# The last two superblocks: products laid out chunk by chunk, summed to one tap group, and transposed by a DMA

## The chip, the cores and the metric

The kernel runs on one core of one Trainium2 chip. The metric is the device time in microseconds, as a median over several runs; lower is better. Profile times are those of one profiled execution.

## The reference

A dynamic convolution over tokens, followed by a two-layer network without gates:

```python
# x: (8, 4096, 192), weight_gen: (8, 4096, 8, 7): 8 heads of 24 channels, 7 taps
w = softmax(weight_gen, axis=-1)                       # one weight per token, head and tap
x_unf = 7 tokens ending at each token, zeros ahead of the first one
conv = np.einsum('bshk,bskhg->bshg', w, x_unf)         # 32768 tokens x 192
h = conv @ w_in                                        # 192 x 2048
out = (h - np.tanh(h)) @ w_out                         # 2048 x 192, float32
```

## The kernel before

The 32768 tokens are cut into 32 superblocks of 1024 (`TOK`), numbered n = 0 to 31. Within a superblock partition p holds `J` = 8 neighbouring tokens, so a tap's products are 8 x 192 = 1536 elements on each of 128 partitions. The 192 channels are split over `NC` = 3 chunks of `R` = 64 rows each: channel d = 3u + c is row u of chunk c.

A superblock passes through these stages:

- *Softmax.* ScalarE takes the exponential of the weights, VectorE sums, inverts and scales them into `wsm`.
- *Products* (`products`, and its inner `mul` and `rest`). GpSimd multiplies x by the weights: taps 0 to 3 into the tile `pa` (two instructions, one less token block for taps 0 and 1, which VectorE does in `help`), then taps 4 to 6 into `pb` (one instruction). Products are bf16, written in the order of x: token, then channel.
- *Sums by DMA* (`dma_sum`, issued from GpSimd's queue, adding in the destination). The first adds `pb` to three tap groups of `pa`. From superblock 13 on (`TWO_SUMS`), `second_sum` adds two of the remaining four groups to the other two. It is issued in the next superblock's turn, between that one's `pa` and `pb` products; that of the last superblock comes right behind its first sum.
- *Transposes* (`transposes`, `conv_sums`, `conv_out`). TensorE multiplies each remaining tap group, 64 rows by 64 columns at a time, by an identity, adding the groups up in PSUM (`pc`, line 384): with two groups 32 matmuls for chunks 0 and 1, and 16 for chunk 2. ScalarE evicts the two results to `convT` (line 410).
- *First matmul* (`gemm1`, line 427). For each of 16 tiles f of the 2048 hidden units, 6 matmuls of 512 columns into `ph`; ScalarE takes the tanh of it into `th` (line 440), VectorE writes `ph - th` to `gt` (line 441).
- *Second matmul* (`out_stream`, line 495). It lags by one superblock: 8 output blocks of 16 pairs of matmuls each go to two PSUM banks, and ScalarE evicts each block (`store_out`, line 514); SyncE stores a superblock's result in one DMA (line 518). The last superblock's second matmul runs at the end (`gemm2_last`).

The order on every engine is written out by hand: TensorE and the others follow the loop over n and f at the end of the code. A plan for n says how many output pairs follow each tile f (`pairs`), and behind which tile, after how many pairs, the transposes of superblock n+1 are put (`t2` for chunks 0 and 1, `t1` for chunk 2):

```python
STEADY = dict(pairs=(5, 11, 0, 16, 4, 12, 6, 10, 0, 6, 10, 8, 8, 8, 8, 16), t1=(14, 8), t2=(13, 0), scale=14, sums=(1, 13))
```

In turn n GpSimd makes the products of superblock n+2 (`pa` at f = 1, `rest` at f = 3), so superblock 30 is multiplied in turn 28 and 31 in turn 29. Loads of x and of the weights and the stores are DMAs of SyncE's queue. `pa` has three buffers, `pb` one, `convT` two, and `ph` and `pc` share three.

Of the kernel before, what the change touches and what calls it, by code (L numbers as in the profile page):

```python
# [9 lines left out]
BF16 = mybir.dt.bfloat16  # L10

ACT = mybir.ActivationFunctionType
# [4 lines left out]
def kernel(  # L17
# [8 lines left out]
    nc = tc.nc  # L26

    B, S, D = x.shape
    H, K = weight_gen.shape[2], weight_gen.shape[3]
    G = D // H  # L30
    F = moe_w_in.shape[1]
    P = nc.NUM_PARTITIONS
    R = P // 2
    HALO = K - 1

    J = 8
    TOK = P * J
    JH = J // 2
    HT = TOK // 2
# [3 lines left out]
    NC = D // R  # L43
    KA, KH = 4, 2
    PART = (2, 3)
    TWO_SUMS = (13, 14, 15, 16, 17, 18, 19, 20, 21, 22, 23, 24, 25, 26, 27, 28, 29, 30, 31)
    AHEAD = 4
    STORE_FIRST = 8
    EXTRA = (5, 9, 11, 13)
# [17 lines left out]
    cpool = ctx.enter_context(tc.tile_pool(name="cpool", bufs=2))  # L67
# [24 lines left out]
    prods_of = {}  # L92
    to_sum = {}
    conv_of = {}
    g_of = {}
    last_act = {}
    probe = {}
# [96 lines left out]
    def softmax_norm(n, bank):  # L194

        wsm = softmax_tile()
        zr_v = bank[:, 512 - J * H : 512]
        nc.vector.reciprocal(zr_v, zsum_of[n][:])  # L198

        def finish():  # L200
            scale(nc.vector, wsm[:], e_of[n], zr_v)

        wsm_of[n] = (wsm, None, None, None)
        return finish
# [30 lines left out]
    def dma_sum(out, in_):  # L235
        return nc.gpsimd.dma_start(  # L236
            out=out.rearrange("p k j d -> p k (j d)"),
            in_=in_.rearrange("p k j d -> p k (j d)"),
            accum_op=mybir.AluOpType.add,
            max_dma_last_dim=2 * J * D,  # L240
        )

    def help(n, ph, j):

        if n not in held:
            held[n] = (x_of[n], wsm_of[n][0], papool.tile([P, KA, J, D], BF16, name="pa"))
        x_t, wsm, pa = held[n]
        x_v = x_t[:]
        w = ph[:, 0, 0 : KH * H].rearrange("p (k h) -> p k h", k=KH)
        nc.vector.tensor_copy(w, wsm[:, j].rearrange("p h k -> p k h")[:, 0:KH])  # L250
        nc.vector.tensor_mul(  # L251
            pa[:, 0:KH, j, :].rearrange("p k (h g) -> p k h g", h=H),
            bass.AP(
                tensor=x_v.tensor,
                offset=x_v.offset + j * D,
                ap=[x_v.ap[0], [D, KH], [G, H], [1, G]],
            ),
            w.rearrange("p k (h o) -> p k h o", o=1).to_broadcast([P, KH, H, G]),
        )

    def products(n, taps=None, sums=None, hooks={}):

        x_t = x_of.pop(n)
        wsm, wsm_v, e_t, zr = wsm_of.pop(n)
        if e_t is not None:
            scale(nc.gpsimd, wsm[:], e_t, zr[:])

        pa = held[n][2] if n in held else papool.tile([P, KA, J, D], BF16, name="pa")
        held[n] = (x_t, wsm, pa)
        if n == 1:  # L270

            last = [opool.tile([P, 2, J, D], BF16, name="pb1", tag="out_sb") for _ in range(2)]
            home = [(pa, 0, KA), (last[0], KA, KA + 2), (last[1], KA + 2, K)]
        else:
            pb = pbpool.tile([P, K - KA, J, D], BF16, name="pb")
            home = [(pa, 0, KA), (pb, KA, K)]
        x_v = x_t[:]
        step = x_v.ap[0]

        def prod(k0, k1):  # L280
            for t, a, b in home:
                if a <= k0 and k1 <= b:
                    return t[:, k0 - a : k1 - a]

        def mul(eng, k0, k1, j0=0, j1=J):

            if eng is nc.scalar:
                for j in range(j0, j1):
                    for h in range(H):
                        eng.activation(  # L290
                            out=prod(k0, k1)[:, 0, j, h * G : (h + 1) * G],
                            in_=x_t[:, k0 + j, h * G : (h + 1) * G],
                            func=ACT.Copy,
                            scale=wsm[:, j, h, k0 : k0 + 1],
                        )
                return
            w = wsm_v if eng is nc.vector else wsm[:]
            nj = j1 - j0
            return eng.tensor_mul(  # L299
                prod(k0, k1)[:, :, j0:j1].rearrange("p k j (h g) -> p k (j h) g", h=H),  # L300
                bass.AP(
                    tensor=x_v.tensor,
                    offset=x_v.offset + (k0 + j0) * D,
                    ap=[step, [D, k1 - k0], [G, nj * H], [1, G]],
                ),
                w[:, j0:j1]
                .rearrange("p j h (k o) -> p k (j h) o", o=1)[:, k0:k1]
                .to_broadcast([P, k1 - k0, nj * H, G]),
            )

        def parts(*ks):
            return [[prod(k, k + 1)[:, 0] for k in ks]] * NC

        if taps is not None:
            for eng, k0, k1, j0, j1 in taps:
                m = mul(eng, k0, k1, j0, j1)
                if eng is nc.vector:
                    tap_of.setdefault((n, k0), m)
                if j1 == 1:
                    first_halo[0] = m  # L320
                if k0 in hooks:
                    hooks[k0]()
            prods_of[n] = parts(*sums)
            return

        nt = len(HELP.get(n, ()))
        first = mul(nc.gpsimd, 0, KH, 0, J - nt)
        if n in PACED:

            order(first, pace_of[n - 3], "pace")  # L330
        if n in LAST_TAP:

            x_after[n + 1] = mul(nc.gpsimd, KH, KA - 1)
            second_sum(n - 1)
        else:
            mul(nc.gpsimd, KH, KA)
            second_sum(n - 1)
        if n not in LAST_TAP or n not in X_LATE:
            x_after[n + 1] = first

        def rest():
            if n in PART:
                dma_sum(pa[:, 0:2], pa[:, 2:4])
            mul(nc.gpsimd, KA, K)
            if n in PART:
                prods_of[n] = parts(4, 5, 6, 0, 1)
            else:
                dma_sum(pa[:, 0:3], pb[:, 0:3])
                if n in LAST_TAP:
                    mul(nc.gpsimd, KA - 1, KA)  # L350
                if n in TWO_SUMS:
                    to_sum[n] = pa
                    prods_of[n] = parts(0, 1)
                else:
                    prods_of[n] = parts(3, 0, 1, 2)
                if n == NTOT - 1:
                    second_sum(n)

        return rest

    def second_sum(n):

        if n in to_sum:
            pa = to_sum.pop(n)
            dma_sum(pa[:, 0:2], pa[:, 2:4])

    def conv_sums(n, parts, pcs, home=None):

# [154 lines left out]
    pairs = out_stream()  # L523
# [68 lines left out]
    for c in range(NC):  # L592
# [16 lines left out]
        sums=(6, 5, 4, 3, 0, 2, 1),  # L609
# [17 lines left out]
    if SOFT_EARLY:  # L627
# [6 lines left out]
        sums=(0, 1, 4, 5, 6, 2, 3),  # L634
# [19 lines left out]
    for f in range(NFT):  # L654
# [9 lines left out]
        if f == EARLY[0][0]:  # L664
            pcs = []
            sums = conv_sums(1, ((0, 1),), pcs, obank)
# [15 lines left out]
    STEADY = dict(pairs=(5, 11, 0, 16, 4, 12, 6, 10, 0, 6, 10, 8, 8, 8, 8, 16), t1=(14, 8), t2=(13, 0), scale=14, sums=(1, 13))  # L682
    FIRST = dict(pairs=(4, 12, 0, 16, 1, 15, 0, 16, 0, 16, 0, 13, 3, 0, 16, 16), t1=(15, 2), t2=(11, 10), scale=15, sums=(1, 2, 3, 4, 8, 10))
    APART = dict(pairs=(4, 12, 0, 16, 0, 16, 4, 12, 0, 16, 4, 12, 0, 6, 10, 16), t1=(15, 5), t2=(10, 2), scale=15, sums=(7, 10))
    APART_IN = ()
    DOUBLE = dict(pairs=(4, 12, 0, 16, 0, 16, 5, 11, 0, 5, 11, 6, 10, 0, 16, 16), t1=(15, 4), t2=(11, 4), scale=15, sums=(1, 10))
    DOUBLE_IN = (4, 5, 6, 7, 8, 9, 10, 11)

    def transposes(n, chunks):
        pcs = []  # L690
# [16 lines left out]
    for n in range(1, NTOT):  # L707
        more = n < NTOT - 1
        finish = []
        plan = FIRST if n == 1 else DOUBLE if n in DOUBLE_IN else APART if n in APART_IN else STEADY  # L710

        soft = [m for m in (n + 3 if n <= AHEAD else n + 4,) if m < NTOT]
        for f in range(NFT):
            ph = gemm1(n, f)
# [37 lines left out]
            for chunks, at in sorted((((0, 1), plan["t2"]), ((2,), plan["t1"])), key=lambda c: c[1]):  # L752
                if more and at[0] == f:
                    out_pairs(at[1] - done)
                    done = at[1]
                    pc = transposes(n + 1, chunks)
                    if chunks == (2,):
                        finish = [softmax_norm(m, pc[:, 0]) for m in soft]
            if f >= plan["scale"]:
                for scale_one in finish:  # L760
                    scale_one()
                finish = []
# [42 lines left out]
```

## Time and profile before

| What | us |
|---|---|
| median of 3 runs | 746.24 (745.77 to 746.59) |
| span of the profiled execution (its own time from first to last instruction) | 743.4 |
| TensorE busy in it | 722.3 (97%) |
| VectorE, ScalarE, GpSimd busy | 687.4, 638.8, 654.5 |
| granted TensorE clock, mean | 0.995 of full speed |
| one matmul of line 427, of line 495 (duration, overlapping its neighbours) | 0.379, 0.243 |
| the chain that ended last | TensorE 92%, VectorE 5%, the rest 3% |

Matmuls are pipelined, so their durations overlap; the chain of waits, which gives how far each group moves the end, shows 0.65 us for the 6 matmuls of a tile and 1.32 us for the 32 of an output block. A superblock's stage is the time from its first matmul of line 427 to that of the next; stages 28, 29 and 30 take 21.85, 21.90 and 21.81 us.

### The profile page before, as it was taken

How to read it: one execution, taken by the hardware profiler on the slowest of the kernel's cores; microseconds unless marked ns; L12 is line 12 of the kernel's file. 1: busy time of each engine (PE TensorE's matmuls, PEld its weight loads, DVE VectorE, ACT ScalarE, POOL GpSimd, SP SyncE). 2: the span in 40 equal slices, each digit the busy share in tenths (PEclk: the TensorE clock that was granted, in tenths of full speed). 3: DMA queues.
4: the chain of work that ended last, by engine and by line, in shares of the span. 5: the costliest groups of instructions: out<-in, count | busy, mean ns of one | idle time of the engine just before them, and what ended most of it. 6: DMA issues, size and time to landing. Idle time of an engine off the chain costs nothing.

```text
span 743.4 us, 30037 instructions
## 1 busy us (share of the span) xinstructions
PE 722.3 (97%) x13616; PEld 556.5 (75%) x13616; DVE 687.4 (92%) x723; ACT 638.8 (86%) x872; POOL 654.5 (88%) x163
## 2 busy tenths in 40 slices
PE   3899999999999999999999999999999999999997
PEld 2477777778777777777777777777777777877777
DVE  7999899999999999999999999999999999988893
ACT  4888888888888888989889999898998989888882
POOL 7999999999999999999999999999999999991000
PEclk9899999999999999999999999999999999999999
DMA  8925367766567668878777977877887877776112
GB/s 236 245 46 161 135 172 185 195 179 149 124 183 184 183 185 224 210 199 203 166 202 209 236 186 204 178 195 205 221 209 195 192 181 194 193 149 110 45 45 86
DMA packets 34269, 130.06 MB, mean 175 GB/s; under 512 B 4591, under 2 KB 9439, under 8 KB 30174
## 3 DMA queue, kind: packets, MB, share of 16 engines
q0 software_dynamic: 19424, 51.12, 40.4%
q1 hardware_dynamic: 14718, 77.03, 27.6%
q8 instruction: 106, 1.74, 0.9%
q14 instruction: 21, 0.17, 0.1%
HBM read 54.52 MB, written 25.17 MB: 107 GB/s over the span
## 4 chain that ended last, share of the span: by engine, by line
PE 92%; DVE 5%; ACT 1%; issue 1%; DMA 1%; SPq 0%; DVEq 0%
PE ph L427 43%; PE obank L495 43%; PE pc L384 4%; DVE gt L441 3%; PE po L538 1%; ACT th L440 1%; DVE pa L299 1%; DMA wg_t<-in_weight_gen_dram 1%; DVE zsum L183 0%; SPq L134 0%; ACT convT L402 0%; DVE obank L211 0%; DVE pa L251 0%; DVE pb L299 0%; SPq L144 0%
## 5 line engine op out<-in xcount | busy, mean ns | idle before, releaser
L441 DVE TENSOR_TENSOR gt<-ph,th 128x1024 bf16<-128x1024 f32 x512 | 601.6, 1217 | 33.4 <-ACT th L440 23.2
L440 ACT ACTIVATE th<-ph 128x1024 f32<-128x1024 f32 x512 | 512.1, 1025 | 69.2 <-PE ph L427 60.3
L427 PE MATMUL ph<-convT,w_in 64*128 64x512 bf16 x3072 | 415.1, 379 | 5.3 <-DVE gt L441 3.3
L495 PEld LDWEIGHTS <-gt 64*128 64x128 bf16 x7936 | 355.6, 94 | 80.6 <-issue 6.3
L495 PE MATMUL obank<-w_out,gt 64*128 64x192 bf16 x7936 | 408.0, 243 | 0.9 <-issue 0.8
L299 POOL TENSOR_TENSOR pa<-x_t,wsm 128x2688 bf16<-128x2688 f32 (+3 forms) x68 | 338.9, 5232 | 0.2
L299 POOL TENSOR_TENSOR pb<-x_t,wsm 128x4608 bf16<-128x4608 f32 (+2 forms) x33 | 283.8, 8601 | 0.7 <-ACT wsm L221 0.5
L427 PEld LDWEIGHTS <-w_in 64*128 64x128 bf16 x3072 | 163.0, 94 | 86.0 <-issue 18.3
L514 ACT ACTIVATE out_sb<-obank 128x192 f32<-128x192 f32 x248 | 81.3, 328 | 11.2 <-PE obank L495 10.3
L410 ACT ACTIVATE convT<-pc 128x1024 bf16<-128x1024 f32 (+1 forms) x62 | 50.1, 810 | 2.9 <-PE pc L384 2.7
L236 POOL DMA_DIRECT2D pa<-pb x28 | 36.0, 1284 | 13.7 <-POOL pb L299 9.1
L384 PEld LDWEIGHTS <-pa 64*128 64x128 bf16 x2064 | 41.5, 100 | 6.8 <-DVE pa L299 1.1
L236 POOL DMA_DIRECT2D pa<-pa x21 | 34.7, 1651 | 9.6 <-DMA pa<-pb 8.9
L384 PE MATMUL pc<-ident,pa 64*128 64x64 bf16 x1968 | 41.2, 191 | 1.8 <-POOL pa L299 0.9
L183 DVE TENSOR_REDUCE zsum<-wg_t 128x32 f32<-128x224 f32 (+1 forms) x61 | 23.6, 387 | 2.9 <-ACT wg_t L169 2.9
L169 ACT ACTIVATE wg_t<-wg_t 128x448 f32<-128x448 f32 x32 | 18.2, 570 | 6.3 <-DMA wg_t<-in_weight_gen_dram 6.2
L251 DVE TENSOR_TENSOR pa<-x_t,ph 128x384 bf16<-128x384 f32 x34 | 18.8, 554 | 2.0 <-DVE ph L250 0.3
L229 DVE TENSOR_TENSOR wsm<-wg_t,pc 128x448 f32<-128x448 f32 x27 | 16.8, 621 | 2.5
L198 DVE RECIPROCAL pc<-zsum 128x64 f32<-128x64 f32 x27 | 14.9, 550 | 0.0
L384 PE MATMUL pc<-ident,pb 64*128 64x64 bf16 x216 | 4.9, 206 | 9.0 <-POOL pb L299 9.0
L384 PEld LDWEIGHTS <-pb 64*128 64x128 bf16 x288 | 6.3, 106 | 9.5 <-POOL pb L299 9.0
L538 PE MATMUL po<-w_out,gt 64*128 64x192 bf16 x256 | 11.2, 243 | 0.0
(27 smaller groups left out, 56.8 us busy)
## 6 DMA issues: line engine op xcount, KB each, us to landing
x_t<-in_x_dram SPq DMA_DIRECT2D x31, 1344.0 KB, 7.9
pa<-pb POOLq DMA_DIRECT2D x28, 1152.0 KB, 9.5
out_dram<-out_sb SPq DMA_DIRECT2D x31, 768.0 KB, 3.9
pa<-pa POOLq DMA_DIRECT2D x21, 768.0 KB, 7.2
wg_t<-in_weight_gen_dram SPq DMA_DIRECT2D x32, 224.0 KB, 7.1
x_t<-in_x_dram SPq DMA_DIRECT2D x1, 768.0 KB
w_out<-in_moe_w_out_dram POOLq DMA_DIRECT2D x1, 768.0 KB, 9.5
out_dram<-out_sb SPq DMA_DIRECT2D x4, 192.0 KB, 3.0
```

The costliest lines, as they stand in the source:

```text
L183: nc.vector.reduce_sum(out=zsum_of[n][:, j0 * H : j1 * H], in_=e_of[n][:, j0:j1].rearrange("p j h k -> p (j h) k"), axis=AX.X,)
L236: return nc.gpsimd.dma_start(out=out.rearrange("p k j d -> p k (j d)"), in_=in_.rearrange("p k j d -> p k (j d)"), accum_op=mybir.AluOpTyp ...
L251: nc.vector.tensor_mul(pa[:, 0:KH, j, :].rearrange("p k (h g) -> p k h g", h=H), bass.AP(tensor=x_v.tensor, offset=x_v.offset + j * D, ap= ...
L299: return eng.tensor_mul(prod(k0, k1)[:, :, j0:j1].rearrange("p k j (h g) -> p k (j h) g", h=H), bass.AP(tensor=x_v.tensor, offset=x_v.offs ...
L384: nc.tensor.matmul(pc[r][:, col : col + R] if home else pc[:, r, col : col + R], lhsT=prods[c][gi][r * R : (r + 1) * R, 2 * j : 2 * j + 2] ...
L410: last_conv[0] = nc.scalar.activation(out=out, in_=pc[:, :, 0:cols].rearrange("p r (cj t) -> p r cj t", t=R), func=ACT.Copy,)
L427: nc.tensor.matmul(ph[:, r, :], lhsT=w_in[r * R : (r + 1) * R, c, f * P : (f + 1) * P], rhs=convT[r * R : (r + 1) * R, c, :], start=(c == ...
L440: last_act[0] = nc.scalar.activation(out=th[:], in_=ph_f, func=ACT.Tanh)
L441: last_sub[0] = nc.vector.tensor_sub(gt[:], ph_f, th[:])
L495: mm = nc.tensor.matmul(po[:, 0:D], lhsT=g_of[n][f][r * R : (r + 1) * R, col : col + P], rhs=w_out[r * R : (r + 1) * R, f, :], start=(r == ...
L514: last_act[0] = nc.scalar.activation(out=out_sb[:, j, :], in_=po[:, 0:D], func=ACT.Copy)
L538: nc.tensor.matmul(po[:, r, 0:D], lhsT=g_of[n][f][r * R : (r + 1) * R, col : col + P], rhs=w_out[r * R : (r + 1) * R, f, :], start=(f == 0 ...
```

## The change

For superblocks 30 and 31 (`THREE`):

- A product instruction writes chunk by chunk: the tap's 1536 elements go to [chunk][token block][row], so neighbouring channels land 512 elements apart. What it reads is unchanged. `help` writes its share in the same way. All other superblocks get the instructions that they had.
- `third_sum`, one more accumulating DMA of GpSimd's queue, adds the second of the two remaining tap groups to the first. Superblock 30's is queued behind 31's `pb` product and ahead of its first sum; 31's comes last on that queue.
- `turn` issues a transposing DMA from SyncE's queue, which brings the one tap group (128 partitions x 1536) into `convT` as 12 blocks of 128 x 128. It waits for the third sum. It takes the place of the matmuls with the identity and their two evictions, in turns 29 and 30.
- The plan of turns 29 and 30 is `TURNED`: no transposes on TensorE, and the output pairs are spread a little differently; 128 as before. In the queue of SyncE the transpose is put behind the store that is issued in the same turn.

```diff
+    THREE = (30, 31)
...
+    def tap_product(eng, n, out, x_t, w, w_step, k0, k1, j0, j1):
+
+        nk, run = k1 - k0, (j1 - j0) * H
+        x_v = x_t[:]
+        if n in THREE:
+            n_in = (j1 - j0) * R
+            to = [[1, n_in], [J * R, NC]]
+            of = [[NC, n_in], [1, NC]]
+            first = j0 * R
+        else:
+            to = of = [[G, run], [1, G]]
+            first = j0 * D
+        return eng.tensor_mul(
+            bass.AP(tensor=out.tensor, offset=out.offset + first, ap=[out.ap[0], [J * D, nk], *to]),
+            bass.AP(tensor=x_v.tensor, offset=x_v.offset + (k0 + j0) * D, ap=[x_v.ap[0], [D, nk], *of]),
+            bass.AP(tensor=w.tensor, offset=w.offset, ap=[w.ap[0], [w_step[0], nk], [w_step[1], run], [0, G]]),
+        )
...
@@ help
-        nc.vector.tensor_mul(
-            pa[:, 0:KH, j, :].rearrange("p k (h g) -> p k h g", h=H),
...
+        tap_product(nc.vector, n, pa[:, 0:KH], x_t, w, (H, 1), 0, KH, j, j + 1)
...
@@ products: mul
-            return eng.tensor_mul(
-                prod(k0, k1)[:, :, j0:j1].rearrange("p k j (h g) -> p k (j h) g", h=H),
...
+            return tap_product(eng, n, prod(k0, k1), x_t, w[:, j0:j1, :, k0:k1], (1, K), k0, k1, j0, j1)
...
@@ products: rest
             else:
+                third_sum(n - 1)
                 dma_sum(pa[:, 0:3], pb[:, 0:3])
...
                 if n == NTOT - 1:
                     second_sum(n)
+                    third_sum(n)
...
@@ second_sum
             dma_sum(pa[:, 0:2], pa[:, 2:4])
+            if n in THREE:
+                whole[n] = pa
+
+    def third_sum(n):
+
+        if n in whole:
+            pa = whole[n]
+            dma_sum(pa[:, 0:1], pa[:, 1:2])
+
+    def turn(n):
+
+        pa = whole.pop(n)
+        conv_of[n] = cpool.tile([P, NC, HT], BF16, name="convT")
+        nc.sync.dma_start_transpose(
+            out=conv_of[n][:].rearrange("p c (j t) -> p (c j) t", t=P),
+            in_=pa[:, 0].rearrange("p j d -> p (j d)"),
+        )
...
+    TURNED = dict(pairs=(5, 11, 0, 16, 3, 13, 6, 10, 0, 6, 10, 5, 11, 5, 11, 16), t1=(16, 0), t2=(16, 0), scale=14, sums=(1, 7))
+    TURN_AT = 13
...
@@ the loop
-        plan = FIRST if n == 1 else DOUBLE if n in DOUBLE_IN else APART if n in APART_IN else STEADY
+        turned = n + 1 in THREE
+        plan = TURNED if turned else FIRST if n == 1 else DOUBLE if n in DOUBLE_IN else APART if n in APART_IN else STEADY
...
+            if turned and f == TURN_AT:
+                turn(n + 1)
+            if turned and f == plan["scale"]:
+                finish = [softmax_norm(m, ph[:, 0]) for m in soft]
```

`soft` is empty in turns 29 and 30, so the last two lines add no instruction.

More of the change, by code (lines that the diff above doesn't have):

```diff
@@ L94 @@
     conv_of = {}
+    whole = {}
     g_of = {}
@@ L247, in help @@
         x_t, wsm, pa = held[n]
-        x_v = x_t[:]
         w = ph[:, 0, 0 : KH * H].rearrange("p (k h) -> p k h", k=KH)
         nc.vector.tensor_copy(w, wsm[:, j].rearrange("p h k -> p k h")[:, 0:KH])
-        nc.vector.tensor_mul(
-            pa[:, 0:KH, j, :].rearrange("p k (h g) -> p k h g", h=H),
[L253 to L259, printed above, removed]
+        tap_product(nc.vector, n, pa[:, 0:KH], x_t, w, (H, 1), 0, KH, j, j + 1)
     def products(n, taps=None, sums=None, hooks={}):
@@ L276, in products @@
             home = [(pa, 0, KA), (pb, KA, K)]
-        x_v = x_t[:]
-        step = x_v.ap[0]
         def prod(k0, k1):
@@ L285, in mul @@
         def mul(eng, k0, k1, j0=0, j1=J):
[L287 to L296, printed above, removed]
-            w = wsm_v if eng is nc.vector else wsm[:]
-            nj = j1 - j0
-            return eng.tensor_mul(
-                prod(k0, k1)[:, :, j0:j1].rearrange("p k j (h g) -> p k (j h) g", h=H),
[L301 to L309, printed above, removed]
+            w = wsm_v if eng is nc.vector else wsm[:]
+            return tap_product(eng, n, prod(k0, k1), x_t, w[:, j0:j1, :, k0:k1], (1, K), k0, k1, j0, j1)
         def parts(*ks):
```

## The prediction

> **What bounds the kernel now.** I read the page's busy shares first, then the busy times by stage, then the chain of waits, and last the queues of GpSimd and of the DMAs around the last two superblocks.
>
> ```profile
> PE 722.3 (97%) x13616; PEld 556.5 (75%) x13616; DVE 687.4 (92%) x723; ACT 638.8 (86%) x872; POOL 654.5 (88%) x163
> ```
>
> Over the span TensorE is busiest. The stages are cut at the first matmuls of superblocks 28, 29, 30 and 31 (columns: stretch, its length, busy us and instructions of PE, PEld, DVE, ACT, POOL, then granted clock, DMA share, GB/s):
>
> ```profile
> 640.55:662.40 21.85, 21.85 (x405) 17.60 (x402) 20.03 (x20) 19.31 (x26) 21.31 (x6) 1.00 0.61 127
> 662.40:684.30 21.90, 21.90 (x406) 17.28 (x403) 19.49 (x18) 19.41 (x27) 10.33 (x3) 1.00 0.69 142
> 684.30:706.11 21.81, 21.81 (x406) 16.87 (x402) 18.94 (x16) 19.32 (x27) 0.00 (x0) 1.00 0.22 61
> ```
>
> TensorE has no gap in any of them, so a matmul taken out there shortens the kernel. GpSimd is as full in stage 28, half used in stage 29, and has nothing to compute in stage 30. The chain of waits shows what TensorE does from the end of stage 29 into stage 30 (start, us, what):
>
> ```profile
> 679.73 0.47 PE pc L384 x32
> 680.20 0.66 PE obank L495 x16
> 680.86 0.76 PE ph L427 x6
> 681.62 0.66 PE obank L495 x16
> 682.27 0.23 PE pc L384 x16
> 682.51 0.65 PE ph L427 x6
> 683.16 1.32 PE obank L495 x32
> 684.48 0.65 PE ph L427 x6
> ```
>
> The `pc` lines are the transposes of superblock 30; the last line is its first use. The GpSimd queue meanwhile (superblock 31's products from 649.66, superblock 30's second sum at 660.13, 31's first sum at 670.73, its second at 680.96):
>
> ```profile
> 638.96 9.34 POOL L299 TENSOR_TENSOR pb<-x_t,wsm 128x4608 bf16<-128x4608 f32 x1
> 649.66 11.02 POOL L299 TENSOR_TENSOR pa<-x_t,wsm 128x2688 bf16<-128x2688 f32 x2
> 660.13 1.73 POOL L236 DMA_DIRECT2D pa<-pa  x1
> 660.90 9.33 POOL L299 TENSOR_TENSOR pb<-x_t,wsm 128x4608 bf16<-128x4608 f32 x1
> 670.73 1.28 POOL L236 DMA_DIRECT2D pa<-pb  x1 [0.50 <-POOL pb L299]
> 680.96 1.21 POOL L236 DMA_DIRECT2D pa<-pa  x1 [8.95 <-DMA pa<-pb]
> ```
>
> **Removed: 96 matmuls and 4 evictions.** Each stage loses 32 + 16 transposing matmuls, 0.47 + 0.23 = 0.70 us, and two evictions on ScalarE (1.62 us, off the path). The matmuls behind the first group take 0.76 us where such a group elsewhere takes 0.65, so a little more may go: 16 groups at 0.65 and 8 output blocks at 1.32 make 20.96 us, 0.94 and 0.85 below the two stages. From below: superblock 31 has no transposes, and in the chain its first to last L427 groups lie 19.23 us apart (706.29 to 725.52) against 19.84 in stage 30, only 0.61 less. I take 0.75 per stage, between the ends, so **1.5 us** for both (1.2 to 1.8). The redistributed output pairs are 128 as before and cost nothing; VectorE at 19.5 us and ScalarE at under 18 stay below a 21.1 us stage.
>
> **Moved: what the first matmul waits for.** It now needs a third sum and a DMA transpose. TensorE runs in order, so nothing behind that matmul can fill a wait: each us of lateness is a us of time. Superblock 30's deadline is 684.48 - 0.75 = 683.7; superblock 31's is 706.29 - 1.5 = 704.8.
>
> **Added: the third sums.** The DMA issues of the page (KB, median us from issue to landing):
>
> ```profile
> pa<-pb POOLq DMA_DIRECT2D x28, 1152.0 KB, 9.5
> out_dram<-out_sb SPq DMA_DIRECT2D x31, 768.0 KB, 3.9
> pa<-pa POOLq DMA_DIRECT2D x21, 768.0 KB, 7.2
> out_dram<-out_sb SPq DMA_DIRECT2D x4, 192.0 KB, 3.0
> ```
>
> From 768 to 1152 KB a sum gains 2.3 us, so one of 384 KB lands in 4.9. Superblock 30's is queued on GpSimd behind 31's `pb` product, which ends at 660.90 + 9.33 = 670.2; its own input, issued at 660.13, has landed by 667.3. It lands at 675.1. Behind it in the queue stands 31's first sum: 1.2 us later (the 1.21 us issue), so issued at 671.9 and landed at 681.4. Its second sum (issued about 0.8 us later, 7.2) lands at 689.4 and its third at 694.3.
>
> **Added: the transposes.** No row shows one. On SyncE's queue the transpose of superblock 30 holds only the store of `out_sb`, which is issued at 687.49 now, so that wait is free. Call the transpose T. It may take up to 683.7 - 675.1 = 8.6 us for superblock 30 and 704.8 - 694.3 = 10.5 for 31. Near bounds: a plain DMA of twice its bytes lands in 3.9 us, one of half in 3.0. The diff writes runs of 128 bf16, 256 bytes, so 128 x 12 = 1536 pieces, 96 for each of 16 DMA engines. The nearest small pieces are those of the `w_out` load (384 bytes in bf16); the queues from 24.2 to 32 us (packets, MB, share of 16 engines):
>
> ```profile
> q0 software_dynamic: 1971, 0.75, 80.6%
> ```
>
> 0.806 x 7.8 x 16 / 1971 = 51 ns per piece, so 4.9 us more, T = 7.9. A far bound, if each 256 byte run broke into eight: 39 + 3 = 42 us. I take T = 6, between 3.9 and 7.9, because the pieces are nearest to these rows: 681.1, with 2.6 us to spare. [...]
>
> **Changed: how the products are written.** The same elements are read in the same order, but neighbours now go to places 512 elements apart. Four stretches of GpSimd stand ahead of superblock 30's third sum (two `pa` pairs, two `pb`): 11.01 + 9.34 + 11.02 + 9.33 = 40.7 us. Bounds: nothing, since reads, multiplies and count stay, or the slowest GpSimd product per element in the trace (min/median/max ns):
>
> ```profile
> L299 POOL TENSOR_TENSOR pb<-x_t,wsm x33: 2893/9316/9350, 6.0 to 660.9; 128x4608 bf16<-128x4608 f32 x30, 128x1536 bf16<-128x1536 f32 x2, 128x3072 bf16<-128x3072 f32 x1
> L229 POOL TENSOR_TENSOR wsm<-wg_t,zr x2: 1402/1434/1467, 51.6 to 156.1; 128x448 f32<-128x448 f32 x2
> ```
>
> 1434/448 = 3.20 ns against 9316/4608 = 2.02: 58% more, 23.6 us. I take nothing, since the same instruction on the same operands is the nearer row. A gain is ruled out of the sum: an earlier product would only wait longer. The two VectorE products (0.55 us each) could even double: VectorE has 21.85 - 20.03 = 1.8 us free in stage 28.
>
> **Sum.** -1.5 us and no stall. The page's span is 743.4, and the page has no other time of that execution; the median of the runs is 746.24, 2.8 around the span. Neither end is touched, so 746.24 - 1.5 = 744.7. About 0.2%, 1.5 us, is what a measurement of this kernel can tell from no change, so this forecast stands just at that line.
>
> **Rivals.**
> 1. *GpSimd's scattered writes are slower* (ends slower). It decides from 2.6 / 40.7 = 6.4% more per element. At half the bound, 29%, superblock 30 is 11.8 us later, 9.2 past its deadline; 31's deadline moves along, so nothing is added: 744.7 + 9.2 = 753.9. For it: 2.6 us is little. Against: the instruction takes 2.02 ns per element with two operands to read and one to write, so the write need not be what it is paced by. [...] Chance 0.22.
> 2. *The transpose is slow by itself* (slower). It decides from T = 8.6. At 16, twice the near upper bound, the stall is 7.4: 752.1; superblock 31 adds none, 16 being under 10.5 + 7.4. Against: it lies beyond every plain row. [...] Chance 0.15.
> 3. *The transpose shares the engines with 31's first sum*, which holds them until 681.4. If all the pieces wait for that, they end at 681.4 + 4.9 = 686.3, 2.6 late: 747.3; between this and the forecast, 746.0. For it: that sum stands right behind on the same 16 engines. Chance 0.15, mostly no change.
>
> **Chances.** Forecast 0.48, split at the line: 0.27 faster, 0.21 no change. Rival 3: 0.10 no change, 0.05 slower. Rivals 1 and 2: 0.37 slower. So faster 0.27, same 0.31, slower 0.42. The forecast's own range is 744.4 to 745.0, 744.0 with the spread of the runs (0.4). Upward the range takes in rivals 3 and 2 and rival 1 up to its middle, 754. That leaves out the upper half of rival 1 and the tail of rival 2, under 0.2.
>
> **What would show it.** In the chain: no `pc` pieces in stages 29 and 30, and those stages at about 21.1 us. For each step: the `pb` product of superblock 31 still at 9.3 us; the third sums at some 4.9 us to landing; the transposes at about 6; the first L427 group of superblock 30 without idle time before it. I am wrong if TensorE idles there: waiting for the DMA with products at 9.3 us means rival 2 or 3 (told apart by whether the transpose of 31, alone on the engines, is as slow); with products over 9.9 us, rival 1.

## The result: 54 us slower, and the profile after

The changed kernel takes 800.16 us (median of 5 runs, 798.79 to 800.88) against 746.24: a ratio of 1.0725, 95% interval 1.0709 to 1.0741. The profiled execution spans 798.8 us, 55.4 more than before. The page's busy times:

```profile
PE 723.8 (91%) x13520; PEld 555.0 (69%) x13520; DVE 689.9 (86%) x723; ACT 636.3 (80%) x868; POOL 711.2 (89%) x165
```

GpSimd has 57 us more to do with two instructions more; the other engines do what they did. By stages, cut as before at the first matmuls of superblocks 28 to 31 and the end (columns as before: stretch, length, busy us of PE, PEld, DVE, ACT, POOL, granted clock, DMA share, GB/s):

```profile
640.36:665.05 24.69, 22.06 (x406) 16.55 (x403) 21.44 (x20) 19.48 (x27) 24.69 (x4) 1.00 0.43 121
665.05:738.13 73.08, 21.36 (x357) 15.98 (x353) 21.86 (x19) 18.40 (x26) 62.83 (x9) 0.69 0.35 65
738.13:761.83 23.70, 23.70 (x353) 16.96 (x355) 17.67 (x16) 17.83 (x23) 0.91 (x2) 0.88 0.46 102
761.83:798.80 36.97, 33.41 (x629) 27.94 (x624) 22.98 (x25) 21.37 (x34) 0.00 (x0) 0.99 0.17 66
```

Stage 28 is 2.8 us longer, stage 29 51.2, stage 30 1.9, the rest as before. In stage 29 TensorE has its 21 us of work and idles for the remainder. GpSimd's queue holds what TensorE waits for (superblock 30's products from 627.61 and 654.18, 31's from 677.05 and 703.35, 30's third sum at 723.68):

```profile
627.61 26.55 POOL L257 TENSOR_TENSOR pa<-x_t,wsm 128x2688 bf16<-128x2688 f32 x2
653.40 1.62 POOL L238 DMA_DIRECT2D pa<-pa  x1
654.18 21.76 POOL L257 TENSOR_TENSOR pb<-x_t,wsm 128x4608 bf16<-128x4608 f32 x1
676.24 1.29 POOL L238 DMA_DIRECT2D pa<-pb  x1 [0.30 <-POOL pb L257]
677.05 26.47 POOL L257 TENSOR_TENSOR pa<-x_t,wsm 128x2688 bf16<-128x2688 f32 x2
702.57 1.80 POOL L238 DMA_DIRECT2D pa<-pa  x1
703.35 21.82 POOL L257 TENSOR_TENSOR pb<-x_t,wsm 128x4608 bf16<-128x4608 f32 x1
723.68 2.02 POOL L238 DMA_DIRECT2D pa<-pa  x1
```

In the kernel before, the same products took 11.0 and 9.3 us. The four stretches add up to 96.6 us against 40.7: 2.4 times, 55.9 us more, all of it ahead of superblock 30's third sum. TensorE's waits (engine and line, what it waited for: us, times, longest), and two issues from SyncE's queue:

```profile
PE ph L433 <- DMA convT<-pa: 50.5, 1, 50.5
PE ph L433 <- DVE pa L257: 2.4, 2, 1.2
PE pc L390 <- DMA pa<-pa: 1.5, 1, 1.5
```

```profile
728.89 5.06 SPq L368 DMA_TRANSPOSE convT<-pa  x1
749.80 1.44 SPq L368 DMA_TRANSPOSE convT<-pa  x1
```

The 50.5 us stand ahead of superblock 30's first matmul. The other two lines are stage 28's loss and a little of stage 29's. VectorE's scattered share of the products takes 1.97 us instead of 0.55 (superblock 29's, in the order of x, and then 31's), and it stands ahead of the `gt` that frees TensorE's next `ph`:

```profile
625.69 0.55 DVE L257 TENSOR_TENSOR pa<-x_t,ph 128x384 bf16<-128x384 f32 x1
672.26 1.97 DVE L257 TENSOR_TENSOR pa<-x_t,ph 128x384 bf16<-128x384 f32 x1
```

The third line is superblock 29's second sum, which is queued behind 30's slow `pa` products (653.40 instead of 638.18).

### The profile page after: what moved, and what is told of

Its sections match the earlier page's. It is cut to its first block, busy times and chain, and to the rows that moved or that the text cites. A ratio compares the mean times of both kernels' runs of the same rounds, so it can differ in the third digit from the quotient of the medians.

```text
span 798.8 us, 29849 instructions
## 1 busy us (share of the span) xinstructions
PE 723.8 (91%) x13520; PEld 555.0 (69%) x13520; DVE 689.9 (86%) x723; ACT 636.3 (80%) x868; POOL 711.2 (89%) x165
## 4 chain that ended last, share of the span: by engine, by line
PE 71%; POOL 18%; DVE 4%; issue 4%; DMA 3%; ACT 1%; POOLq 0%; DVEq 0%; SPq 0%
PE ph L433 33%; PE obank L501 33%; POOL pa L257 10%; POOL pb L257 6%; PE pc L390 3%; DVE gt L447 2%; POOL pa L238 1%; PE po L544 1%; DMA convT<-pa 1%; ACT th L446 1%; DMA x_t<-in_x_dram 1%; DMA pa<-pa 1%; DVE pa L257 0%; DMA wg_t<-in_weight_gen_dram 0%; DVE pb L257 0%
## 5 line engine op out<-in xcount | busy, mean ns | idle before, releaser
L433 PE MATMUL ph<-convT,w_in 64*128 64x512 bf16 x3072 | 416.2, 380 | 58.7 <-DMA convT<-pa 50.5
L257 POOL TENSOR_TENSOR pa<-x_t,wsm 128x2688 bf16<-128x2688 f32 (+3 forms) x68 | 369.8, 5695 | 0.2
L257 POOL TENSOR_TENSOR pb<-x_t,wsm 128x4608 bf16<-128x4608 f32 (+2 forms) x33 | 308.4, 9347 | 1.2 <-DVE gt L447 0.4
L238 POOL DMA_DIRECT2D pa<-pa x23 | 37.5, 1629 | 16.1 <-DMA pa<-pb 10.0
L416 ACT ACTIVATE convT<-pc 128x1024 bf16<-128x1024 f32 (+1 forms) x58 | 46.9, 811 | 3.8 <-PE pc L390 3.7
L390 PEld LDWEIGHTS <-pa 64*128 64x128 bf16 x1968 | 39.3, 100 | 7.9 <-issue 1.9
L390 PE MATMUL pc<-ident,pa 64*128 64x64 bf16 x1872 | 38.9, 191 | 3.1 <-DMA pa<-pa 1.5
L185 DVE TENSOR_REDUCE zsum<-wg_t 128x32 f32<-128x224 f32 (+1 forms) x61 | 23.6, 387 | 2.9 <-ACT wg_t L171 2.9
L257 DVE TENSOR_TENSOR pa<-x_t,ph 128x384 bf16<-128x384 f32 x34 | 21.7, 638 | 2.0 <-DVE ph L269 0.3
```

What stands on the lines that cost most here:

```text
L185: nc.vector.reduce_sum(out=zsum_of[n][:, j0 * H : j1 * H], in_=e_of[n][:, j0:j1].rearrange("p j h k -> p (j h) k"), axis=AX.X,)
L238: return nc.gpsimd.dma_start(out=out.rearrange("p k j d -> p k (j d)"), in_=in_.rearrange("p k j d -> p k (j d)"), accum_op=mybir.AluOpTyp ...
L257: return eng.tensor_mul(bass.AP(tensor=out.tensor, offset=out.offset + first, ap=[out.ap[0], [J * D, nk], *to]), bass.AP(tensor=x_v.tensor ...
L390: nc.tensor.matmul(pc[r][:, col : col + R] if home else pc[:, r, col : col + R], lhsT=prods[c][gi][r * R : (r + 1) * R, 2 * j : 2 * j + 2] ...
L416: last_conv[0] = nc.scalar.activation(out=out, in_=pc[:, :, 0:cols].rearrange("p r (cj t) -> p r cj t", t=R), func=ACT.Copy,)
L433: nc.tensor.matmul(ph[:, r, :], lhsT=w_in[r * R : (r + 1) * R, c, f * P : (f + 1) * P], rhs=convT[r * R : (r + 1) * R, c, :], start=(c == ...
```

## Experiments

My theory after the result: A, the scattered 2-byte writes are the whole loss. The rivals: the added DMAs, the layout that they read, or some other part of the new access patterns.

**The scattered products alone.** No third sum, no DMA transpose; TensorE transposes from the new layout:

```diff
-            if n in THREE:
-                whole[n] = pa
...
+        if n in THREE:
+            flat = rows.rearrange("p j d -> p (j d)")
+            first = (c * J + 2 * j) * R
+            return flat[:, first : first + 2 * R]
...
-        turned = n + 1 in THREE
+        turned = False
```

> The scattered products of superblocks 30 and 31 alone: no third sum, no DMA transpose; TensorE transposes their two tap groups as in the kernel before, reading the chunk-by-chunk layout (128 contiguous columns each). Theory A, the scattered writes are the cause: the GpSimd products of 31 and 30 take 26.5 and 21.8 us as in the changed kernel (11.0 and 9.3 before), so superblock 30's second sum lands near 709.6 us instead of 667 and its transposes stall TensorE by about 30 us (709.6 against 679.7); superblock 31's second sum lands near 742 and stalls the next stage by about 10 us more; with a slower clock after the stall some 40 to 43 us in all: about 787 to 790. Rival B, the third sums and the transposing DMA are the cause: the products may be slow but the time stays within 5 us of the kernel before, about 746 to 751.

788.77 us, ratio 1.0565 (1.0534 to 1.0596), 42.3 us over the kernel before: within theory A. Its waits, and the two stretches of superblock 31:

```profile
PE pc L396 <- DMA pa<-pa: 34.3, 3, 26.1
```

```profile
678.39 26.44 POOL L257 TENSOR_TENSOR pa<-x_t,wsm 128x2688 bf16<-128x2688 f32 x2
704.67 21.84 POOL L257 TENSOR_TENSOR pb<-x_t,wsm 128x4608 bf16<-128x4608 f32 x1
```

TensorE now waits for the second sums; nothing of the new DMAs is needed for most of the loss. The other 12 us of the change have their place in the queue: its third sum for superblock 30 stands behind 31's `pb` product, another 21.8 us.

**Which pattern costs.** Ten, then eight more products of 1536 elements (or fewer) on GpSimd behind its last sum and on VectorE behind its last addition. They write to spare tiles that nothing reads; the kernel is else the one before:

```diff
+        e.tensor_mul(ap(spare, 0, (1, 1536)), X, W)
+        e.tensor_mul(ap(spare, 0, (1, 512), (512, 3)), X, W)
...
+        e.tensor_mul(ap(spare, 0, (64, 8), (512, 3), (1, 64)), X, W)
+        e.tensor_mul(ap(wide, 0, (1, 1536)), X, W)
+        e.tensor_mul(ap(wide, 0, (1, 512), (512, 3)), X, W)
...
+    patterns(nc.gpsimd)
```

> The kernel before, with ten extra products of 1536 elements each on GpSimd behind its last sum, and the same ten on VectorE behind its last addition; they write to spare tiles that nothing reads, so the time of this kernel says nothing, only the duration of each line. Written as [step, count] from outer to inner: contiguous; [1,512][512,3] as in the change; [1,768][768,2]; [4,512][1,3]; [2,1536]; [4,1536]; runs of 64 [64,8][512,3][1,64]; float32 contiguous; float32 [1,512][512,3]; and contiguous writes with x read as [1,3][3,512]. Contiguous should take 3.0 us on GpSimd. Theory A1, each bf16 write far from its neighbour costs: 1536 x 4.7 ns = 7.2 us for the change's pattern, as much for [1,768][768,2], about 3.0 for [4,512][1,3], [2,1536], [4,1536] and the runs of 64; on VectorE 5 to 7 us against 1.7. Rival A2, runs of three are what costs: [4,512][1,3] takes 7.2 too and [1,768][768,2] even more, runs of 64 3.0. Rival A3, only writes of less than a word pay, because neighbours in the same word are no longer written together: float32 [1,512][512,3] stays near its contiguous form (under 20% more) while [2,1536] and [4,1536] in bf16 are slow.

The timeline of GpSimd and VectorE: the change's pattern (L784), runs of 64 (L789), the change's pattern in float32 (L791):

```profile
685.78 7.08 POOL L784 TENSOR_TENSOR pa<-x_t,wsm 128x1536 bf16<-128x1536 f32 x1
709.84 2.90 POOL L789 TENSOR_TENSOR pa<-x_t,wsm 128x1536 bf16<-128x1536 f32 x1
715.68 2.95 POOL L791 TENSOR_TENSOR x_t<-x_t,wsm 128x1536 f32<-128x1536 f32 x1
742.92 7.01 DVE L784 TENSOR_TENSOR pa<-x_t,wsm 128x1536 bf16<-128x1536 f32 x1
767.67 2.79 DVE L791 TENSOR_TENSOR x_t<-x_t,wsm 128x1536 f32<-128x1536 f32 x1
```

It is not the far place by itself (on GpSimd float32 goes to places as far in 2.95 us) and not runs of three (2.90 and 1.76 us in the table below). Two engines that need about 2.9 and 1.75 us for writes that keep their neighbours both take 7.0. Theory A1 missed one row: a step of 8 bytes took 3.67 us where it had 3.0. The second set:

> Eight more write patterns on GpSimd and on VectorE at the end of the kernel before; only the durations of its lines count. In bf16 768 elements contiguous, with steps of 4 (8 bytes) and of 8 (16 bytes); 1536 elements in runs of 2, 4 and 8 neighbours that go to places 512 elements apart; 512 float32 contiguous and with a step of 4 (16 bytes). Theory W, a write of less than 4 bytes far from the last one costs, whole words do not: runs of 2 take about 3.0 us on GpSimd, as runs of 4 and 8, and the float32 step of 16 bytes is near contiguous. Theory L, what counts is a new 16-byte line: runs of 2 lie between (about 4 to 5 us), runs of 4 below that, runs of 8 at 3.0; the float32 step of 16 bytes is slow too. In both the bf16 step of 16 bytes costs more than that of 8.

768 elements with a step of 16 bytes (L790), and 1536 in runs of two neighbours, each run at a far place (L791):

```profile
687.37 3.67 POOL L790 TENSOR_TENSOR pa<-x_t,wsm 128x768 bf16<-128x768 f32 x1
691.12 2.91 POOL L791 TENSOR_TENSOR pa<-x_t,wsm 128x1536 bf16<-128x1536 f32 x1
744.92 3.56 DVE L790 TENSOR_TENSOR pa<-x_t,wsm 128x768 bf16<-128x768 f32 x1
748.51 1.76 DVE L791 TENSOR_TENSOR pa<-x_t,wsm 128x1536 bf16<-128x1536 f32 x1
```

All of both runs, in us:

| written as [step, count], outer to inner | elements | GpSimd | VectorE |
|---|---|---|---|
| bf16 contiguous | 1536 | 3.37 (the first of the ten) | 1.75 |
| bf16 [1,512][512,3], the change | 1536 | 7.08 | 7.01 |
| bf16 [1,768][768,2] | 1536 | 7.10 | 6.93 |
| bf16 [4,512][1,3], runs of three | 1536 | 2.90 | 1.76 |
| bf16 step 4 bytes | 1536 | 2.91 | 1.86 |
| bf16 step 8 bytes | 1536 | 3.67 | 3.56 |
| bf16 step 8 bytes (contiguous) | 768 | 1.93 (2.01, the first of the eight) | 1.86 (0.95) |
| bf16 step 16 bytes | 768 | 3.67 | 3.56 |
| bf16 runs of 2, 4, 8 at far places | 1536 | 2.91, 2.91, 2.90 | 1.76, 1.76, 1.76 |
| bf16 runs of 64 at far places | 1536 | 2.90 | 1.76 |
| float32 contiguous, [1,512][512,3] | 1536 | 2.90, 2.95 | 1.75, 2.79 |
| float32 step 16 bytes (contiguous) | 512 | 1.17 (1.16) | 1.06 (0.68) |
| bf16 contiguous, x read with a step of 12 bytes | 1536 | 3.61 | 2.17 |

Lone 2-byte writes cost 4.5 to 4.8 ns for each stretch of 16 bytes that they open, on either engine: 7.08/1536 for the far places, 3.67/768 for a step of 16 bytes, and at a step of 8 bytes, with two in each stretch, again 3.67 for 768 stretches. This price is not added to the time of the multiplication, for then the two engines would differ (7.08 and 7.01 us for the far places, 2.90 and 1.76 for runs of 64); the longer of the two counts in these rows. So, as an estimate from these rows, a step of 4 bytes opens 384 stretches for 1.8 us, which GpSimd's 2.9 us hide and which VectorE shows (1.86 us). Theory L does not hold: two neighbours that fill one word of 4 bytes are free at a far place (2.91 and 1.76 us, as runs of 64). Theory W holds on GpSimd (float32 with a step of 16 bytes 1.17 us against 1.16); on VectorE whole words have a price too, though a smaller one (float32 with a step of 16 bytes 1.06 us against 0.68). Why a lone half word costs that is not shown.

**The change without scattered writes, in every superblock.** Products in runs of 64, chunk by chunk, with w_in's rows in that order and one instruction per tap:

```diff
+        to = [[R, nj], [J * R, NC], [1, R]] if nj > 1 else [[J * R, NC], [1, R]]
+        for k in range(k0, k1, by):
...
-                ap=[[NC * F, R], [F, c1 - c0], [1, f1 - f0]],
+                ap=[[F, R], [R * F, c1 - c0], [1, f1 - f0]],
```

The control has `THREE = ()`, the next kernel `(30, 31)`, the last `(31,)`.

> Control for the next two: every superblock's products are written chunk by chunk with 64 neighbouring channels to a chunk (runs of 128 bytes), one instruction per tap, and the rows of w_in follow; no third sum, no DMA transpose, TensorE transposes as before. If runs of 64 cost nothing, as the pattern run has it (2.90 us for 1536 elements), and seven instructions cost what three did, it is the kernel before: 745 to 748 us. Rival: each extra instruction costs GpSimd 0.1 us or more; its 21.3 us of a 21.85 us stage then pass the stage and it comes out 5 to 12 us slower.

753.11 us, ratio 1.0096 (1.0083 to 1.0109): 7 us slower, as the rival had it. A superblock's products take 11.28 + 9.60 us instead of 11.02 + 9.33. That these 0.5 us cause the loss is not shown: stages 28 to 30 last 21.8 to 21.9 us as before, the time is lost in single earlier stages, and the waits of TensorE that grew most are put down to issue (3.5 us in five waits ahead of the second matmul, against 0.8 in two before).

> The change in full (third sums, DMA transposes and the TURNED plan for superblocks 30 and 31) but with the products in runs of 64, so without scattered writes. Theory A, the scattered writes are the whole of the loss: the products of 31 take 11.0 and 9.3 us again, stages 29 and 30 shrink by 0.75 us each, and what is left is rival 3 of the prediction: superblock 30's transpose is issued near 675 us, its packets wait for 31's first sum (over near 681) and it lands at 683 to 685 against a deadline of 683.7. So 0 to 1.5 us faster than the control. Rival B, the transposing DMA is too slow even then: a wait of over 3 us ahead of superblock 30's first matmul, and no faster than the control.

758.14 us, ratio 1.0167 (1.0150 to 1.0184), 5 us over the control; theory A's forecast of a small gain missed, and the wait of over 3 us that rival B had is there. 42 of the 54 us are gone, though, and TensorE's waits show what is left in stage 29:

```profile
PE ph L429 <- DMA convT<-pa: 4.3, 1, 4.3
```

GpSimd had fallen behind here: superblock 31's `pa` products begin 12.7 us into stage 28 (660.41, with the stage from 647.70), 9.1 before. That is 3.6 us of lateness. It explains about half of the 4.3: the kernel further down that has runs of 64 in two superblocks only is hardly late there and still waits 2.2 us.

> The same with the third sum and the DMA transpose for superblock 31 alone. Nothing else is on the DMA engines then (the transpose of 31 took 3.3 us in the changed kernel) and its slack was 10 us: 0.6 to 0.9 us faster than the control, no wait ahead of superblock 31's first matmul.

749.83 us, ratio 1.0055 (1.0032 to 1.0078), in runs from 747.5 to 753.7 against 750.0 to 753.8 of the control: 3.3 us between the medians where 0.6 to 0.9 were expected, and too wide a spread to tell 0.8 us. In the profile stage 30 takes 21.00 us, and nothing waits ahead of superblock 31's first matmul.

**Contiguous writes instead of contiguous reads.** The change in full, the same places, but the elements in another order: chunk after chunk, x read with a step of 12 bytes, with one instruction per tap, in superblocks 30 and 31 alone:

```diff
-            to = [[1, n_in], [J * R, NC]]
-            of = [[NC, n_in], [1, NC]]
+            for k in range(nk):
+                ... ap=[out.ap[0], [J * R, NC], [1, n_in]]
+                ... ap=[x_v.ap[0], [1, NC], [NC, n_in]]
+                ... ap=[w.ap[0], [0, NC], [w_step[1], run], [0, G // NC]]
```

> The change in full with only the order of the products' elements altered in superblocks 30 and 31: chunk after chunk, contiguous writes, x read with a step of 12 bytes, one instruction per tap. Theory A, writes of 2 bytes that each open a new place are the loss: the products take 0.7 us more per tap than before (3.61 against 2.90), 10 us over both superblocks, so superblock 30's transpose is 8 to 10 us past its deadline: 752 to 755 us, some 46 of the 54 us gone. Rival B, the loss is in the sums and transposes or in the layout that they read: it stays over 780.

755.59 us, ratio 1.0135 (1.0118 to 1.0152): 0.6 us over the expected range. 44 of the 54 us are gone, with the same places written in another order. GpSimd (superblock 31's products) and the wait:

```profile
654.77 13.79 POOL L252 TENSOR_TENSOR pa<-x_t,wsm 128x1344 bf16<-128x1344 f32 x4
668.83 11.63 POOL L252 TENSOR_TENSOR pb<-x_t,wsm 128x1536 bf16<-128x1536 f32 x3
```

```profile
PE ph L436 <- DMA convT<-pa: 9.5, 1, 9.5
```

The four stretches of products take 51.0 us, 10.3 more than in the kernel before, and TensorE waits 9.5: what the products are late comes back as waiting.

**The same for superblock 31 alone** (`THREE = (31,)`):

> Third sum and DMA transpose for superblock 31 alone; its products go to the same chunk-by-chunk places as in the change, but chunk after chunk, so writes are contiguous and x is read with a step of 12 bytes; one instruction per tap, in superblock 31 only. By the pattern run (3.61 against 2.90 us per tap) its products take some 5 us longer, of about 10 us of slack; the DMA transpose alone on the engines takes 3.3 us. Theory A: no wait ahead of superblock 31's first matmul, stage 30 at 21.0 us, 0.8 us faster than the kernel before: 745.4. Rival: the products come so late that second sums and the transpose miss the deadline: slower than before.

745.29 us, ratio 1.0000 (0.9990 to 1.0009), no difference that can be measured. Stage 30 in its windows:

```profile
687.53:708.53 21.00, 21.00 (x358) 16.19 (x355) 18.81 (x17) 18.05 (x25) 2.11 (x2) 1.00 0.52 115
```

21.00 us without a gap, 0.81 less than before: the saving is there, below what the times resolve.

**Runs of 64 in the two superblocks only**, with a second copy of w_in for them:

```diff
+    w_runs = const.tile([P, NC, F], BF16, name="w_runs")
...
-                    lhsT=w_in[r * R : (r + 1) * R, c, f * P : (f + 1) * P],
+                    lhsT=(w_runs if n in THREE else w_in)[r * R : (r + 1) * R, c, f * P : (f + 1) * P],
```

> The change in full with products in runs of 64 channels for superblocks 30 and 31 only (one instruction per tap there), every other superblock as before, and a second copy of w_in with its rows in that order, loaded by two DMAs of GpSimd's queue in turns 13 and 16. From the control run a superblock's products take 20.9 us against 20.35, so the third sum of 30 is 1.1 us later than I reckoned and its transpose, which waits for 31's first sum on the engines, lands 1 to 2 us past the deadline: stages 29 and 30 at 22 to 23 and 21.0 us; against 1.6 us saved, 745 to 747 us (the two loads may add up to 1). Rival: the transpose of 30 is as slow as in the changed kernel (9.2 us) also here: a wait of 3 us or more.

749.17 us, ratio 1.0044 (1.0032 to 1.0057); 2 us more than I expected, but of the 53.9 us of the change only 3.2 are left. Its wait for superblock 30's transpose, and two of the windows after that wait:

```profile
PE ph L438 <- DMA convT<-pa: 2.2, 1, 2.2
```

```profile
688.00:690.00 2.00, 2.00 (x24) 1.34 (x20) 1.23 (x1) 1.57 (x2) 0.00 (x0) 0.54 0.93 169
690.00:692.00 2.00, 2.00 (x22) 1.20 (x18) 1.23 (x1) 0.53 (x3) 0.87 (x1) 0.61 0.01 2
```

The idle 2.2 us cost more than themselves: the granted clock falls to a half for 3.4 us from 688.2, 1.4 us after the wait was over, and stage 30 takes 22.67 us instead of 21.00. In the changed kernel it falls to a half 4.9 us into the wait of 50.5 us (692.5) and stays there for 51.2 us, to 743.7: it slows the first 5.6 us of stage 30, in which TensorE is busy throughout. What sets the start and the length of the half clock is not shown.

**The transpose ahead of 31's first sum**, which then waits for it:

```diff
+                before_it = turn(n - 1) if n - 1 in whole else None
+                first_sum = dma_sum(pa[:, 0:3], pb[:, 0:3])
+                if before_it is not None:
+                    order(first_sum, before_it, "the transpose alone")
```

> As the run before (the change in full with products in runs of 64 for superblocks 30 and 31), but 31's first sum is issued only when superblock 30's transpose has landed, and that transpose is put into SyncE's queue ahead of the stores of its turn. If rival 3 of the prediction is what makes superblock 30's transpose take 7.4 to 8.9 us from issue to its last packet (3.2 to 3.5 us for 31's), it takes 3.2 to 3.6 us now, lands near 681 us, and superblock 30's first matmul no longer waits: stage 29 at 21.0 to 21.2 us. Superblock 31's chain then starts some 9 us later (first sum issued near 681 instead of 672) and its transpose lands near 709, so the wait moves to superblock 31, 3 to 5 us: 748 to 751 us in all. If instead the first transpose of a run is slow by itself, it still takes 7 us or more.

745.25 us, ratio 0.9996 (0.9985 to 1.0006). Superblock 30's transpose in SyncE's queue, first of the kernel before this one, then of this:

```profile
677.40 3.94 SPq L373 DMA_TRANSPOSE convT<-pa  x1
```

```profile
676.40 1.55 SPq L376 DMA_TRANSPOSE convT<-pa  x1
```

In the first it runs beside 31's first sum: its first packet moves 4.5 us after the issue, its last ends after 7.4. Alone, 1.3 and 3.3 us, and the sum that waits for it is issued 4.3 us after it (680.71). So the sum beside it is the cause, and not that it is the first transpose of the run. The issue on SyncE is longer too (3.94 against 1.55 us), so whether the time goes on the DMA engines or already at the issue is not told apart. Stages 29 and 30 of this kernel:

```profile
662.48:683.56 21.08, 21.08 (x357) 16.65 (x354) 19.36 (x19) 18.14 (x25) 10.81 (x6) 1.00 0.57 124
683.56:705.02 21.46, 21.19 (x358) 16.19 (x353) 19.23 (x17) 18.29 (x25) 2.08 (x2) 1.00 0.77 158
```

Together 1.2 us less than in the kernel before the change. The 3 to 5 us that I expected to move to superblock 31 did not come: its sums followed in 20.6 us (680.71 to 701.32), and 0.3 us of waiting is left. It is the change as it could be: its last two stages are the shortest of these kernels with two turned superblocks and shorter than before the change, but not by a time that the runs can tell.

## Why the prediction was wrong, by its own steps

- **Changed: how the products are written** is the step that failed. I took nothing, because reads, multiplies and count stay, with 58% more as the far end; it was 137% more, 55.9 us instead of 0 to 23.6. The mechanism was named (rival 1, chance 0.22) and its path to the time was right: with 55.9 us put into rival 1's own sum, 744.7 + 55.9 - 2.6 = 798.0 us, against 800.16 measured. Its size was wrong: no row of the trace wrote lone half words, and the row that I took for the far end differed in other things. A bound that does not contain the new property is no bound. The upper end of the range, 754, came from half of it.
- **Which writes pay**: in the pattern runs lone bf16 writes do, 4.5 to 4.8 ns for each stretch of 16 bytes that they open. Runs of two (2.91 us on GpSimd) and float32 on GpSimd (2.95 against 2.90) go to far places at no cost, and a step of 8 bytes, with two writes to a stretch, still costs (3.56 us against 1.75 on VectorE).
- **The two VectorE products "could even double".** They took 3.6 times as long, and spare time in the stage was the wrong measure: TensorE waited 1.2 us behind each.
- **Removed**: 0.75 us a stage, measured 0.81 (stage 30 of the kernel with superblock 31 alone).
- **The third sums**: 4.9 us, measured 5.2 for 30's (723.68 to 728.89) and a median of 5.6; 6.5 with runs of 64 in two superblocks (670.92 to 677.40).
- **The transpose**: T = 6 was between two cases. Alone 3.2 to 3.5 us to the last packet, beside 31's first sum 7.4 to 8.9, and there TensorE began 9.2 to 9.4 us after the issue (728.89 to 738.13 in the changed kernel, 677.40 to 686.80 with runs of 64 for two superblocks). That is rival 3, and in the kernel with runs of 64 for two superblocks its wait was 2.2 us, where 2.6 was reckoned. So near a figure is partly luck: the products there were 1.1 us longer and the third sum took 6.5 us instead of 4.9, while the transpose did not wait for the whole of 31's first sum (its first packet moved at 681.9; 31's second sum, which waits for that one, was issued at 683.88). Rival 2's 16 us was not seen. Alone on the engines the transpose landed 3.8 us after its issue (superblock 31's, in the kernel that turns it alone with strided reads), where the stores of 192 and 768 KB land in 3.0 and 3.9.
- **"Each us of lateness is a us"** is too low: behind a wait of 2.2 us the halved clock cost 1.7 more.
- **The sum**: without the scattered writes and with the transpose alone on the engines, the two stages give 1.2 us of the 1.5 that I forecast.

## What to carry to other kernels

Ask of a new layout whether writes of 2 bytes lose their neighbours (1536 of them took 7.08 us instead of 2.90 on GpSimd, 7.01 instead of 1.76 on VectorE). Keep runs that fill whole words, which took 2.91 and 1.76 here, or take the stride on the reading side, 3.61 and 2.17. Where a chain feeds an engine that works in the order of its queue, as TensorE did when it idled 50.5 us ahead of one matmul, add up every instruction of the queues ahead of the first use, and price the idle time with the slower clock behind it (1.7 us more behind a wait of 2.2). A transfer that must be early is put ahead of the bulk transfer, not beside it: the transpose ended 3.3 us after its issue ahead of the sum, 7.4 beside it.

## What the runs showed of the hardware that I had not expected

Lone bf16 writes cost 4.5 to 4.8 ns per 16 bytes opened on GpSimd and on VectorE alike, while pairs that fill a word are free (2.91 and 1.76 us for 1536 elements) and float32 costs nothing on GpSimd (2.95 against 2.90) and about 0.7 ns a write on VectorE (2.79 against 1.75 us for 1536). A transpose of 384 KB by DMA, in 1536 packets of 256 bytes, moved in 2.0 us once started (750.99 to 752.99). Next to an accumulating DMA its first packet moved 4.8 us after the issue in the changed kernel and 4.5 with runs of 64 in two superblocks, alone 1.2 (superblock 31's in the changed kernel) and 1.3 (the last experiment).
